# Running sums of logarithms as a float16 and a float32r product in a gated-recurrence kernel

## The chip, the cores and the metric

The kernel runs on one NeuronCore of one Trainium2 chip. The metric is the device time of one execution in microseconds (us). The engines are called by the names of the profile: PE (TensorE; its weight loads are PEld), DVE (VectorE), ACT (ScalarE), POOL (GpSimd) and SP (SyncE, which here only issues DMAs). They run side by side, each in the order of its own instructions, and wait for each other through semaphores.

## The reference, cut to what matters

```python
# 4 batches, 8 heads, 768 tokens, head dimension 48
for t in range(S):
    state = alpha[:, :, t, :, None] * state + einsum('bhd,bhe->bhde', k[:, :, t], v[:, :, t])
    y[:, :, t] = einsum('bhd,bhde->bhe', q[:, :, t], state)
x = y.transpose(0, 2, 1, 3).reshape(3072, 384)
# mixture of experts: 8 experts, 384 -> 1024 -> 384, each row to one expert
logits = x @ w_gate
expert_idx = argmax(logits, axis=1)            # gate_w: that expert's softmax value
for e in range(8):                             # rows sorted by expert
    y_sorted[lo:hi] = maximum(x_sorted[lo:hi] @ w1[e], 0) @ w2[e]
return gate_w[:, None] * y_sorted[inv_perm]
```

The decay `alpha` lies between 0.8 and 1. The product of the decays from one token to another is computed as the exponential of a difference of running sums of logarithms. These running sums are what the change touches.

## The kernel before, in words

The first stage is the recurrence. The 768 tokens are cut into 6 chunks of 128, and a step handles one chunk of one of the 4 batches, all 8 heads at once: 24 steps, of which step `i` has chunk `i // 4` and batch `i % 4`. The second stage is the mixture of experts, one expert after another; the change does not touch it. The order of the instructions of each engine is the order in which the code writes them (`manual_schedule`), so a step's place in the loop at lines 670 to 746 of the program is also its place in each engine's queue.

For a tile `s` (one chunk of one batch) the stage does this:

- `load` (L380): SP issues the loads of `a`, `k`, `q`, `v`, most of them for two tiles at once (384 KB). `loads_for(i)` at the start of a step issues those that fall due: `a` up to the tile whose sum is taken four steps later, `v`, `k` and `q` three and five tiles ahead. The `a` tiles have 4 buffers, `k` and `q` 3.
- `logs` (L388, ACT): `lna`, the logarithm of `a`, 128x384.
- `cums` (L393, PE; L396 and L397, ACT): one float32 matmul with the constant 128x128 matrix `cum_m` (0, 1 and -1) gives the running sums, taken from the middle of the chunk, in the PSUM bank `cum`. ACT reads it twice: `icp` is the exponential of its negative, `cp` its exponential.
- `decay_out` (L410, DMAs from ACT's queue) brings one row of `icp` and `cp` to the four-row tiles `dec`. `decay_rows` (L418, L419, POOL) multiplies them into the first 4 of the 128 rows of `er`, whose other rows stay zero. `decay_cols` (L430, PE) turns `er` by four transposes against the identity, into a bank that shares the tag `cum`; DVE copies the four columns that matter to `E` (L432).
- `operands` (L439, POOL): `k` times `icp` and `q` times `cp`, to one of three buffers `kqb`.
- `transposes` (L449, PE): eight transposes of `kqb`; copied out as `kT` and `qT` by ACT and DVE (L453, L455).
- `scores` (L462, PE), `mask` (L470, DVE: `dA`, `dB`), `scale_state` (L477, POOL: the state times `E`, called `U`), `read_state` (L489, PE), `attend` (L499, PE), `keys_values` (L510, PE), `result` (L518, ACT: `yT`), `add_state` (L528, DVE: `acc`), `rows` (L536, PE: `x`, output and logits in one bank), `logits` (L543, L544, DVE), `gate` (L550, ACT: `gex`), `keep_rows` (L561, ACT: `xs`; L562, SP's store to `x_rows`).

In step `i` PE runs, in this order: scores of `i`; in steps 4, 8, 12, 16 and 20 the four transposes of `decay_cols`; the eight transposes of `i+1`; the running sums of tile `i+5` (while there are tiles left: steps 2 to 18 have one); read_state, attend and keys_values of `i`; rows of `i-1`. ACT runs `yT` of `i-1`, `gex` of `i-2`, the logarithm of tile `i+5`, `kT` of `i+1`, `icp` and `cp` of tile `i+5`, `xs` of `i-2`, and issues the DMAs of `decay_out`. DVE runs logits, `acc`, in decay steps `E`, the two masks, `qT`, the gate weight, and the routing work that `route(i)` gives it. POOL runs operands of `i+2`, `U` of `i+1` or `decay_rows`, and from step 13 on one-hot rows (L291, L292).

Of the kernel before, what the change touches and what calls it, by code (L numbers as in the profile page):

```python
# [7 lines left out]

F32 = mybir.dt.float32
F16 = mybir.dt.float16  # L10
I32 = mybir.dt.int32
U16 = mybir.dt.uint16
AX = mybir.AxisListType.X
AF = mybir.ActivationFunctionType
ALU = mybir.AluOpType
# [4 lines left out]
def kernel(  # L20
# [29 lines left out]
    nc = tc.nc  # L50
    B, H, S, D = q.shape
    C = 128
# [4 lines left out]
    Dm = H * D  # L57
# [4 lines left out]
    D2 = 2 * D  # L62
    DP = 64
    HC = C // 2
    assert NB * C == S and FB * C == F and DB * C == Dm and D <= DP


# [16 lines left out]
    consts = ctx.enter_context(tc.tile_pool(name="consts", bufs=1))  # L84
    ident = consts.tile([C, C], F32)
    cmask = consts.tile([C, C], F32)
    cum_m = consts.tile([C, C], F32)
    kqb = [consts.tile([C, 2, NP, 2, DP], F32, name=f"kqb{i}") for i in range(3)]
    er = consts.tile([C, NP, 2, DP], F32)

# [9 lines left out]
            nc.vector.memset(t[:, :, :, :, D:], 0.0)  # L100

    def second_consts():
        nc.vector.tensor_scalar_mul(iw[:, :, D2:], iw[:, :, D2:], -1.0)
        for i in range(2):
            nc.vector.tensor_copy(
                iw[i * DP : (i + 1) * DP, :, i * D : (i + 1) * D],
                ident[i * DP : (i + 1) * DP, None, i * DP : i * DP + D].to_broadcast([DP, NP, D]),
            )
# [6 lines left out]
    for name, shape, pattern, base, mult in (  # L115
# [9 lines left out]
        iotas[name] = (  # L125
            consts.tile(shape, I32, name=name + "_i"), consts.tile(shape, F32, name=name), pattern, base, mult,
        )
    first_w, key0, thr, kx, first, cols, iota_f, tokv = (iotas[n][1] for n in iotas)
    iota_r = consts.tile([C, C], F16)
    iota_c = consts.tile([C, NC], F16)  # L130

# [94 lines left out]
    early = ctx.enter_context(tc.tile_pool(name="early", bufs=1))  # L226
    oh_r = sm.tile([C, NT, C], F16)
    oh_c = sm.tile([C, NT, NC], F16)

# [50 lines left out]
    def rows_cols(g_):  # L280
        ts = slice(g_ * TG, (g_ + 1) * TG)
        tr, ti = small("tr", (C, TG)), small("ti", (C, 3, TG), I32)
        nc.vector.reduce_sum(tr[:], pr[g_].rearrange("p e t -> p t e"), axis=AX)
# [21 lines left out]
    def place_experts():  # L305
# [17 lines left out]
        nc.vector.reduce_sum(xf[:], aw[:], axis=AX)  # L323
        xe = small("xe", (1, E), I32)
        nc.vector.tensor_copy(xe[:], xf[:])
        pd.update(end=end, place=place, at=at, xe=xe)

    def decode(v, n, name, pool=None):
# [3 lines left out]
        u, gf, sf = (pool.tile([C, n], F32, name=name + k_) for k_ in "ugs")  # L332
        gi, si = (pool.tile([C, n], I32, name=name + k_) for k_ in ("gi", "si"))
        nc.vector.tensor_scalar(gf[:], v, scalar1=0.0, scalar2=float(N + 1), op0=ALU.is_lt, op1=ALU.mult)
# [4 lines left out]

        qb, qf = pool.tile([C, 2, n], I32, name=name + "qb"), pool.tile([C, 2, n], F32, name=name + "qf")  # L340
        nc.vector.tensor_scalar(sf[:], u[:], scalar1=0.0, scalar2=float(2 * N), op0=ALU.is_lt, op1=ALU.mult)
# [22 lines left out]
    with tc.tile_pool(name="ld", bufs=6) as ld, \  # L364
         tc.tile_pool(name="work", bufs=2) as work, \
         tc.tile_pool(name="ps", bufs=1, space=PSUM) as ps:
        st = {s: {} for s in range(NT)}
# [18 lines left out]
        def logs(s):  # L386
            t = work.tile([C, Dm], F32, name="lna", bufs=4)
            nc.scalar.activation(t[:], st[s]["a"].rearrange("s h d -> s (h d)"), AF.Ln)  # L388
            st[s]["lna"] = t

        def cums(s, bank="cum"):
            cum = ps.tile([C, 512], F32, name="cum", tag=bank)
            nc.tensor.matmul(cum[:, :Dm], lhsT=cum_m[:], rhs=st[s]["lna"][:], start=True, stop=True)  # L393
            cp = work.tile([C, Dm], F32, name="cp", bufs=6)
            icp = work.tile([C, Dm], F32, name="icp", bufs=6)
            nc.scalar.activation(icp[:], cum[:, :Dm], AF.Exp, scale=-1.0)  # L396
            nc.scalar.activation(cp[:], cum[:, :Dm], AF.Exp)  # L397
            st[s]["cp"], st[s]["icp"] = cp, icp
# [25 lines left out]
        def pair(t, p):  # L424
            return t[:, p].rearrange("s a d -> s (a d)")

        def decay_cols(c):
            ep = ps.tile([C, NP, C], F32, name="ep", tag="cum")
            for p in range(NP):
                nc.tensor.transpose(ep[:, p, :], pair(er[:], p), ident[:])  # L430
            decay[c] = work.tile([C, NP, B], F32, name="E", bufs=2)
            nc.vector.tensor_copy(decay[c][:], ep[:, :, :B])  # L432

# [96 lines left out]
        def rows(s):  # L530
# [3 lines left out]
            for m in range(NP):  # L534
                for o in (0, HC):
                    nc.tensor.matmul(  # L536
# [28 lines left out]
        def do(f, i, *a):  # L565
            if 0 <= i < NT:
                f(i, *a)
# [4 lines left out]
        def sums_to(i):  # L572
            return {-2: 1, -1: 1, 0: 3, 1: 5}.get(i, -1 if i < 0 else min(i + 5, NT - 1))

        def new_sums(i):
            return range(sums_to(i - 1) + 1, sums_to(i) + 1)

        loaded = dict(a=0, k=0, q=0, v=0)

        singly = {-5: "aakq", -4: "kqav", -3: "akq", -2: "aav", -1: "kq", 0: "avakq", 1: "vkq"}  # L580
# [5 lines left out]
        def loads_for(i):  # L586
            for n in singly.get(i, ""):
                load_next(n, 1)
            if i > 1:
                for n, upto in ("a", sums_to(i + 4)), ("v", i + 3), ("k", i + 5), ("q", i + 5):  # L590
                    while loaded[n] <= min(upto, NT - 1):
                        load_next(n, 2)

# [70 lines left out]
        def route(i):  # L664
            for f, *args in on_vector.get(i, ()):
                if f is slots:
                    args[1] = counted(args[1])
                f(*args)

        for i in range(-4, NT):  # L670
            loads_for(i)
            do(scores, i)
            if i < NT - 1:
                do(result, i - 1)
            do(logits, i - 2)
            if i >= B:
                do(add_state, i - 1)
            do(gate, i - 2)
            if i > 0:
                for s in new_sums(i):  # L680
                    logs(s)
            if i == NT - 1:
                early_turn()
            if 0 < i < NT and i % B == 0:
                decay_cols(i // B)
            do(mask, i, 0)
            do(mask, i, 1)
            if i < B:
                do(add_state, i - 1)
            do(transposes, i + 1)  # L690
            sums = list(new_sums(i))
            for s in sums[:1]:
                cums(s)
            if i < 0:
                for s in sums[1:]:
                    cums(s, "x")
            do(gate_weight, i - 2)
            route(i)
            do(keep_rows, i - 2)
            if len(sums) == 1:  # L700
                decay_out(sums[0])
            if i == -1:
                for s in range(2):
                    decay_out(s)

            if B - 1 <= i < 2 * B - 1:
                decay_out(i + 1, (1,))
            if i == NT - 2:
                si = next(se)[1]
                eg["si"] = lambda j, r: si[:r, j : j + 1]  # L710
            if i == B:
                scale_state(i)
            do(operands, i + 2)
            if i > B and i % B == 0:
                scale_state(i)
            if 0 < i + 1 < NT and (i + 1) % B == 0:
                decay_rows((i + 1) // B)
            elif i >= 0:
                do(scale_state, i + 1)
            one_hots(nc.gpsimd, *on_gpsimd.get(i, ()))  # L720
            do(read_state, i)
            do(attend, i)
            if i == NT - 2:
                result(i)
            if i >= 0 and sums[1:]:
                cums(sums[1])
                for s in sums:
                    decay_out(s, (0,) if i else (0, 1))
            do(keys_values, i)
            if i == NT - 3:  # L730
                held["tok"] = ps.tile([C, NC], F32, name="tok", tag="cum")
                tokens(held["tok"][:], *range((NG - 1) * TG))
                se = early_gather()
            do(rows, i - 1)
            if i in counts_in:
                counts(counts_in[i], counted(i - 1))
            if i < 0:
                for s in new_sums(i + 1):
                    logs(s)
            if i == -3:  # L740
                second_consts()
            if i in (-4, 0, 1):
                for j in {-4: (0, 1, 2), 0: (3,), 1: (4,)}[i]:
                    late_consts(j)
            if 12 <= i < 22:
                fetch_part(groups[0], i - 12)
# [541 lines left out]
    with tc.If(nx > 0):  # L1288
        with tc.For_i(0, nx, 1) as i:
            ex = nc.sync.value_load(xi[0:1, bass.ds(i, 1)], min_val=0, max_val=E - 1)  # L1290
            col = wk.tile([C, 1], F32, name="col")
            nc.vector.tensor_copy(col[:], xx[:, 1, bass.ds(i, 1)])
            m = wk.tile([C, NT], F16, name="m")
            nc.vector.scalar_tensor_tensor(
# [41 lines left out]
```

## Time and profile before

| What | Before |
|---|---|
| Runs, us | 406.01 median (405.68, 406.01, 410.5) |
| Profiled execution, us | 405.81 |
| Its span, first to last instruction, us | 404.1 |
| PE busy, share of the span | 390.1 us, 97% |
| ACT, DVE, POOL busy | 54%, 51%, 36% |
| Mean granted PE clock | 0.988 |
| Matmuls of `cum` (L393) | 48 records, median 488 ns |
| Transposes of `er` (L430) | 20 records, median 273 ns |

A record is one pass of PE. Every float32 matmul of the table shows as two records, a float32 transpose as one. [...]what a pass costs in a dense stretch is read from start to start. In views named by a line (L393 is line 393 of the program), `out<-in` gives the tiles written and read, `x2` the number of records merged, and the bracket at the end the idle time of the engine before it and what ended it. A view by windows gives, for stretches of time, each engine's busy time with its number of instructions, the granted clock, the share of the DMA engines' time and the rate in GB/s. The recurrence takes the span up to some 146 us, the experts the rest.

### The profile page before, as it was taken

How to read it: one execution, taken by the hardware profiler on the slowest of the kernel's cores; microseconds unless marked ns; L12 is line 12 of the kernel's file. 1: busy time of each engine (PE TensorE's matmuls, PEld its weight loads, DVE VectorE, ACT ScalarE, POOL GpSimd, SP SyncE). 2: the span in 40 equal slices, each digit the busy share in tenths (PEclk: the TensorE clock that was granted, in tenths of full speed). 3: DMA queues.
4: the chain of work that ended last, by engine and by line, in shares of the span. 5: the costliest groups of instructions: out<-in, count | busy, mean ns of one | idle time of the engine just before them, and what ended most of it. 6: DMA issues, size and time to landing. Idle time of an engine off the chain costs nothing. (4 is left out here: it accounts for less than half of the span.)

```text
span 404.1 us, 9032 instructions
## 1 busy us (share of the span) xinstructions
PE 390.1 (97%) x3390; PEld 328.9 (81%) x3390; DVE 207.2 (51%) x636; ACT 219.6 (54%) x502; POOL 147.4 (36%) x203
## 2 busy tenths in 40 slices
PE   7999999999999999969999999999999999999994
PEld 4668888888888885859979978988978979979852
DVE  5554545664575665283692483473473483461200
ACT  5565556566665440112665666666666666763640
POOL 5447454688668203770005007007007003012031
PEclk9999999999999999979999999999999999999998
DMA  9999999999874315879346766865856965711311
GB/s 173 188 201 223 195 221 202 227 210 213 202 191 125 118 42 190 300 211 194 88 156 148 195 195 132 246 185 139 246 151 173 237 201 123 189 22 54 58 56 54
DMA packets 153905, 67.44 MB, mean 167 GB/s; under 512 B 136699, under 2 KB 148082, under 8 KB 153860
## 3 DMA queue, kind: packets, MB, share of 16 engines
q1 hardware_dynamic: 148756, 57.13, 59.0%
q0 software_dynamic: 3408, 9.64, 8.4%
q8 instruction: 27, 0.44, 0.5%
q10 hardware_dynamic: 1696, 0.08, 0.3%
q14 instruction: 18, 0.15, 0.1%
HBM read 49.00 MB, written 9.58 MB: 145 GB/s over the span
## 5 line engine op out<-in xcount | busy, mean ns | idle before, releaser
L1021 POOL DMA_INDIRECT out_dram<-zo,sp x25 | 26.0, 1041 | 137.5 <-ACT zo L1046 127.3
L185 DVE TENSOR_TENSOR h_sb<-pB,u 128x208 f32<-128x208 f32 (+6 forms) x56 | 20.2, 360 | 53.4 <-PE pB L909 39.5
L439 POOL TENSOR_TENSOR kqb<-k_sb,icp 128x384 f32<-128x384 f32 x23 | 23.0, 1000 | 36.8 <-PE y L510 17.0
L991 PE MATMUL pC<-h_sb,w 128*128 128x416 f32 (+5 forms) x96 | 33.9, 496 | 0.0
L851 ACT COPY u<-pA 128x208 f32<-128x208 f32 (+6 forms) x68 | 21.2, 312 | 18.5 <-PE pA L974 11.5
L909 PE MATMUL pA<-t,s 128*128 128x208 f32 (+6 forms) x112 | 28.6, 337 | 0.8
L462 PE MATMUL sA<-qT,kT 48*128 48x128 f32 x192 | 27.7, 284 | 0.9 <-DVE qT L453 0.9
L462 PE MATMUL sB<-qT,kT 48*128 48x128 f32 x192 | 27.7, 285 | 0.0
L909 PE MATMUL pA<-xgT,w 128*128 128x208 f32 (+6 forms) x112 | 27.7, 329 | 0.0
L449 PE MATMUL tp<-ident,kqb 128*128 128x128 f32 x192 | 25.9, 278 | 0.6 <-DVE kqb L439 0.6
L793 POOL DMA_INDIRECT xg<-x_rows,gp x25 | 23.9, 956 | 6.9 <-issue 6.8
L991 PEld LDWEIGHTS pC<-h_sb,w 128*128 128x128 f32 x96 | 18.0, 190 | 10.3 <-issue 3.7
L462 PEld LDWEIGHTS sA<-qT,kT 48*128 48x128 f32 x192 | 23.1, 187 | 3.8 <-ACT kT L455 1.1
L543 DVE TENSOR_REDUCE lgn<-x 128x8 f32<-128x32 f32 x23 | 4.4, 191 | 38.3 <-PE x L536 33.4
L920 ACT ACTIVATE h_sb<-h_sb 128x208 f32<-128x208 f32 (+6 forms) x28 | 10.3, 368 | 25.2 <-DVE h_sb L185 22.0
L909 PE MATMUL pB<-t,w 128*128 128x208 f32 (+6 forms) x112 | 23.8, 335 | 0.0
L439 POOL TENSOR_TENSOR kqb<-q_sb,cp 128x384 f32<-128x384 f32 x23 | 23.1, 1004 | 1.4 <-DMA q_sb<-in_q_dram 1.0
L449 PEld LDWEIGHTS tp<-ident,kqb 128*128 128x128 f32 x192 | 20.8, 140 | 3.4 <-issue 1.2
L909 PE MATMUL pC<-xgT,w 128*128 128x208 f32 (+6 forms) x112 | 23.1, 329 | 0.0
L462 PEld LDWEIGHTS sB<-qT,kT 48*128 48x128 f32 x192 | 23.1, 187 | 0.0
L518 ACT COPY yT<-y 128x512 f32<-128x512 f32 x24 | 14.1, 587 | 15.6 <-PE y L510 10.2
L470 DVE TENSOR_TENSOR dA<-sA,cmask 128x512 f32<-128x512 f32 x24 | 16.5, 689 | 11.3 <-PE sB L462 11.1
(256 smaller groups left out, 995.4 us busy)
## 6 DMA issues: line engine op xcount, KB each, us to landing
w<-in_moe_w_dram SPq DMA_DIRECT2D x14, 1536.0 KB
x_rows<-xs SPq DMA_DIRECT2D x24, 192.0 KB
v_sb<-in_v_dram SPq DMA_DIRECT2D x10, 384.0 KB
k_sb<-in_k_dram SPq DMA_DIRECT2D x9, 384.0 KB
q_sb<-in_q_dram SPq DMA_DIRECT2D x9, 384.0 KB
a_sb<-in_alpha_dram SPq DMA_DIRECT2D x8, 384.0 KB
a_sb<-in_alpha_dram SPq DMA_DIRECT2D x8, 192.0 KB
w<-in_moe_w_dram SPq DMA_DIRECT2D x6, 256.0 KB
```

Of the source, the lines that this page charges most:

```text
L185: eng.tensor_tensor(out, a, b, op=ALU.add)
L439: eng.tensor_tensor(by_half(kq[:, i]), d[n].rearrange("s (a p) d -> s a p d", a=2), d[e][:].rearrange("s (a p d) -> s a p d", a=2, p=NP), ...
L449: nc.tensor.transpose(tp[:, p, :], pair(kqb[s % 3][:, i], p), ident[:])
L462: nc.tensor.matmul(t[:, p, :], lhsT=d["kT"][r : r + D, p, :], rhs=d["qT"][r : r + D, p, :], start=True, stop=True,)
L470: nc.vector.tensor_tensor(t[:], d["sc"][i][:], cmask[:, None, :].to_broadcast([C, NP, C]), op=ALU.mult)
L518: nc.scalar.copy(d["yT"][:], y[:, :, : 2 * C].rearrange("r g (j t) -> r g j t", j=2))
L793: nc.gpsimd.indirect_dma_start(out=g["xg"][:r, j, :], out_offset=None, in_=x_d[:, :], in_offset=bass.IndirectOffsetOnAxis(ap=g["gi"](j, r) ...
L851: nc.scalar.copy(t[:, :m], bank["A"][:, :m])
L909: nc.tensor.matmul(out, lhsT=ops[n_][0], rhs=ops[n_][1], start=first and n_ == names[0], stop=True, skip_group_check=True,)
L920: nc.scalar.activation(out(0, 0), out(0, 0), AF.Relu)
L991: nc.tensor.matmul(d2[:, :n], lhsT=w2[:, f, 2 * C :], rhs=h[:, f, :n], start=(f == 0), stop=(f == FB - 1),)
L1021: ins = nc.gpsimd.indirect_dma_start(out=out[:, :], out_offset=bass.IndirectOffsetOnAxis(ap=g["si"](j, r), axis=0), in_=zo[:r], in_offset= ...
```

## The change

For tiles 11 to 23, whose sums fall in steps 6 to 18, the float32 product is split. ACT writes `hi`, the logarithm times 512 rounded to float16, right after the logarithm. DVE writes `lo`, the logarithm minus `hi`/512, as float32r, at the end of the step's routing work. PE adds two products in the bank: `hi` with `cum_h` (`cum_m`/512 in float16) and `lo` with `cum_r` (`cum_m` in float32r). So that DVE has a step for it, the logarithm and `hi` of these tiles are taken one step before the sum, not in the same step; step 5 takes two logarithms, of tiles 10 and 11. The loads of `a` come one step sooner from step 4 on. `decay_cols` turns only the four rows of `er` that hold data, so the moving identity is 4x4 and an output is 128x4. Two constants are made in `second_consts`, on DVE, before the first step.

```diff
+F32R = mybir.dt.float32r
...
+    APART, HS = 11, 512.0
...
+    cum_r = consts.tile([C, C], F32R)
+    cum_h = consts.tile([C, C], F16)
...
     def second_consts():
+        nc.vector.tensor_copy(cum_r[:], cum_m[:])
+        nc.vector.tensor_scalar_mul(cum_h[:], cum_m[:], 1.0 / HS)
...
             nc.scalar.activation(t[:], st[s]["a"].rearrange("s h d -> s (h d)"), AF.Ln)
             st[s]["lna"] = t
+            if s >= APART:
+
+                st[s]["hi"] = work.tile([C, Dm], F16, name="hi", bufs=2)
+                nc.scalar.mul(st[s]["hi"][:], t[:], HS)
+
+        def low_part(s):
+
+            t = st[s]["lo"] = work.tile([C, Dm], F32R, name="lo", bufs=1)
+            nc.vector.scalar_tensor_tensor(
+                t[:], in0=st[s]["hi"][:], scalar=-1.0 / HS, in1=st[s]["lna"][:], op0=ALU.mult, op1=ALU.add,
+            )
 
         def cums(s, bank="cum"):
             cum = ps.tile([C, 512], F32, name="cum", tag=bank)
-            nc.tensor.matmul(cum[:, :Dm], lhsT=cum_m[:], rhs=st[s]["lna"][:], start=True, stop=True)
+            if s < APART:
+                nc.tensor.matmul(cum[:, :Dm], lhsT=cum_m[:], rhs=st[s]["lna"][:], start=True, stop=True)
+            else:
+                nc.tensor.matmul(cum[:, :Dm], lhsT=cum_h[:], rhs=st[s]["hi"][:], start=True, stop=False)
+                nc.tensor.matmul(cum[:, :Dm], lhsT=cum_r[:], rhs=st[s]["lo"][:], start=False, stop=True)
...
             for p in range(NP):
-                nc.tensor.transpose(ep[:, p, :], pair(er[:], p), ident[:])
+                nc.tensor.transpose(ep[:, p, :B], pair(er[:B], p), ident[:B, :B])
...
+        def new_logs(i):
+            return [s for j in (i, i + 1) for s in new_sums(j) if (s >= APART) == (j > i)]
+
...
-                for n, upto in ("a", sums_to(i + 4)), ("v", i + 3), ("k", i + 5), ("q", i + 5):
+                for n, upto in ("a", sums_to(i + 4 + (i > 3))), ("v", i + 3), ("k", i + 5), ("q", i + 5):
...
-                for s in new_sums(i):
+                for s in new_logs(i):
                     logs(s)
...
             route(i)
+            for s in new_logs(i):
+                if s >= APART:
+                    low_part(s)
             do(keep_rows, i - 2)
```

## The prediction

> **What bounds the kernel now.** I read the page first, for the engine that is never idle.
>
> ```profile
> PE 390.1 (97%) x3390; PEld 328.9 (81%) x3390; DVE 207.2 (51%) x636; ACT 219.6 (54%) x502; POOL 147.4 (36%) x203
> PE   7999999999999999969999999999999999999994
> PEclk9999999999999999979999999999999999999998
> ```
>
> The first 14 digits of 40 (10.1 us each) are the recurrence. PE is at 90% or more there but for the first slice. [...]I then took windows whose edges are the first score matmul of each step. These are steps 18 and 19, the last with a running sum and the first without.
>
> ```profile
> core 0: us, PE busy (x) PEld busy (x) DVE busy (x) ACT busy (x) POOL busy (x), PEclk, DMA share, GB/s
> 111.12:116.57 5.45, 5.45 (x91) 4.46 (x91) 3.83 (x18) 3.81 (x9) 1.88 (x3) 1.00 0.63 164
> 116.57:121.36 4.79, 4.79 (x90) 4.19 (x88) 3.25 (x9) 2.55 (x6) 4.71 (x7) 1.00 0.91 225
> ```
>
> Step 18 takes 5.45 us and step 19 4.79. The timeline of PE says where the 0.66 lies (column one is the start):
>
> ```profile
> 112.22 1.09 PE L449 MATMUL tp<-ident,kqb 128*128 128x128 f32 x8
> 113.14 0.81 PE L393 MATMUL cum<-lna,cum_m 128*128 128x384 f32 x2
> 113.89 0.66 PE L489 MATMUL y<-qT,U 48*48 48x128 f32 x16
> ...
> 117.66 1.09 PE L449 MATMUL tp<-ident,kqb 128*128 128x128 f32 x8
> 118.68 0.65 PE L489 MATMUL y<-qT,U 48*48 48x128 f32 x16
> ```
>
> From transposes to read_state it is 1.67 us with the sum and 1.02 without: the sum alone costs 0.65, and nothing else moved. Steps 6, 7, 9, 10, 13, 14 and 15 also take 5.44 to 5.45. So PE's own instructions set the step, and a step without any sum is shorter by the whole of it. What is taken from the sum is taken from the time, until another engine's chain ends later.
>
> The nearest of these is ACT's. Step 14 begins at 88.36:
>
> ```profile
> 89.20 0.51 ACT L388 ACTIVATE lna<-a_sb 128x384 f32<-128x384 f32 x1
> 90.15 0.59 ACT L455 COPY kT<-tp 128x512 f32<-128x512 f32 x1 [0.44 <-PE tp L449]
> 91.29 0.49 ACT L396 ACTIVATE icp<-cum 128x384 f32<-128x384 f32 x1 [0.56 <-PE cum L393]
> 91.68 0.48 ACT L397 ACTIVATE cp<-cum 128x384 f32<-128x384 f32 x1
> 92.05 0.59 ACT L561 ACTIVATE xs<-x,gw 128x384 f32<-128x384 f32 x1
> ```
>
> ACT waits twice for PE: 0.44 us before `kT`, 0.56 before `icp`. `xs` must be done before the next rows, which write the same single bank `x`: it ends at 92.64, rows start at 92.98.
>
> [...]the sum is two records of some 0.32 us each (0.65 together)[...]. No float32r stands in it. [...]
>
> **The change part by part.** *The sum.* One product of 0.644 us becomes two[...]. The second weight load (190 ns as a record[...]) begins while the first product streams, as it does now. That saves 0.32 per step, times 13 steps: 4.2 us. Bounds: at the rate of one float32 pass, 0.32 for the float32r part, it saves 0.16, 2.1 us in all; at two passes it costs 0.16 more than now, 2.1 us. I take the full rate[...].
>
> *The four transposes.* Steps 12 and 16 against their neighbours: 5.89 against 5.44, 0.44 for four transposes, 0.11 each. The moving side shrinks from 128 to 4 columns; the load remains.
>
> ```profile
> L430 PEld LDWEIGHTS ep<-ident,er x20: 138/141/144, 33.1 to 122.7; 128*128 128x128 f32 x20
> L430 PE MATMUL ep<-ident,er x20: 272/273/332, 33.1 to 122.8; 128*128 128x128 f32 x20
> ...
> L393 PEld LDWEIGHTS cum<-lna,cum_m x48: 186/190/337, 4.2 to 113.1; 128*128 128x128 f32 x48
> ```
> ```profile
> 71.04 0.30 PEld L266 LDWEIGHTS x<-pr,lt_strict 128*128 128x128 f32 x2
> 71.26 0.30 PEld L266 LDWEIGHTS x<-pr,ones_sq 128*128 128x128 f32 x2
> ```
>
> L266 moves 8 columns and still needs 0.11 us a record (two in 0.22): its loads set the pace. A transpose's load is 50 ns shorter (141 against 190), so I put its pace at 0.06: four take 0.24, a gain of 0.20. Against that stands a seam: going from scores to transposes costs PE 0.1 us, and the next eight transposes use all rows again. I take 0.12 per decay step, five of them: 0.6 us. Bounds: 0.20 without a seam (1.0), and 0.44 + 0.1, a loss of 0.1 each (-0.5).
>
> *ACT.* `hi` adds one instruction of 0.51 (the row of `lna`) per step right after the logarithm. It fills the 0.44 before `kT`; `kT` starts 0.05 to 0.1 later, and `icp`, which PE releases 0.32 earlier, still finds ACT free because back-to-back instructions overlap by some 0.1. `xs` waits for the gate weight of DVE, ready at 91.70 here, so it can move up 0.3 with `cp`; rows move up 0.32 too. The margin of 0.34 stays within 0.1. Step 18 has 3.81 us of ACT, with `qT` on it; plus 0.51 that is 4.3 of 5.13. Step 5 gets a logarithm and `hi`, 1.0 us, against the same 0.44; its `icp` waits for PE anyhow and is late by at most 0.3. Uncovered, `hi` would cost 0.5 a step. Zero.
>
> *DVE.* `lo` is one 128x384 instruction; DVE's `kqb` product of that size takes 0.56. It is queued ahead of the next step's `lgn`, before which DVE sits idle 1.4 us at the end of step 13 and 2.2 at that of step 14; behind it wait `gex` and the masks. In step 12, which has routing work, DVE is free from some 81.9 to `lgn` at 83.0, so 0.56 fits; the fullest, step 18, gets none. Zero; 0.5 a step if the cover were gone. The two constants, 0.25 each by the copy to `cum_m` (0.24), fall in DVE's 1.03 us of waiting for `iw` at 3.9.
>
> *The earlier logarithm* takes the wait for `lna` off the sum: PE's only idle time put down to it is 0.6 us at 28.1, before the changed steps, so nothing. *The earlier loads:* from step 4 each pair of `a` is issued one step sooner on SP's queue, ahead of a store of `x_rows` that nobody reads before the gathers at 131, and of the small `alpha` row. The next pairs of `v`, `k` and `q` stood behind it already. A pair takes some 1.7 us (384 KB at 225 GB/s). POOL shows when loads were late:
>
> ```profile
> 55.46 1.00 POOL L439 TENSOR_TENSOR kqb<-q_sb,cp 128x384 f32<-128x384 f32 x1 [0.69 <-DMA q_sb<-in_q_dram]
> 59.65 1.00 POOL L439 TENSOR_TENSOR kqb<-k_sb,icp 128x384 f32<-128x384 f32 x1 [2.25 <-PE y L510]
> ```
>
> Up to step 8 POOL waits for loads, 4.8 us before PE needs their product; after it, for PE. The `k` pair of tiles 20 and 21 is issued at 94.39 and first read at 110.07. Two steps move 1.97 MB; in 10.25 us that is 192 GB/s, from step 12 on with two weight pieces of 0.26 MB 243, where windows of 5 us show up to 264. Zero. *POOL* is full in steps 13 and 14 (5.45 of 5.45), with one-hot rows nobody waits for; `decay_rows` ends at 97.45, PE needs it at 100.3. The cut takes 0.3 a step of this 2.9. Zero.
>
> **Sum.** 4.2 + 0.6 = 4.8 us. The profiled execution is 405.81 (span 404.1 and 1.7 around it), so 401.0; it stands 0.2 below the median of 406.01, to which the forecast is **401.2**. The experts' stage is PE-bound but for two gaps and shifts as a whole.
>
> **The rivals.** *Float32r is slower than I take it.* For it: no row shows it. Half rate gives 406.0 - 2.1 - 0.6 = 403.3; two passes 407.5. *The gain is absorbed,* by ACT through `xs` and the bank `x`, or by the loads: the DMA share is near 1.00 in most windows of the recurrence. Then steps stay at 5.45: 405.4. Against it are the margins above. *The clock.* PE idles twice for 1.6 us at 172.6 and 174.7, and the granted clock halves from 175.8 to 182.7, which costs 3.4 us. All this comes 4.8 us earlier[...]: half of it gone gives 399.5, all 397.8, half more 402.9. *Slower:* the scaling by 512 is not in the table set that ACT holds. The one load of a table here takes 1.28 us (L569); two per step and `hi` make 3.1, ACT's 3.81 becomes 6.9, and ACT sets the period: 1.45 x 13 = 19 us, 424. It decides from 1.6 us added to ACT (5.45 - 3.81). Against it: exponential, logarithm, copy with scale and Relu all run on that one load.
>
> **How the numbers follow.** Forecast 0.66 (400.2 to 402.3); float32r slower 0.12; absorbed 0.07; clock 0.10, of which 0.03 under 398; table 0.03; else slower 0.02. A measurement of this kernel tells about 2% from no change, 8.1 us: faster (below 397.9) 0.03, slower 0.04 (the table and half of the last case), within 0.93. The range goes from half of the clock's gain with the best transposes (399.5 - 0.4) to the half rate with the worst (403.3 + 1.1): 399.1 to 404.4. It leaves out the absorbed case, the two-pass rate, the whole clock's gain, the table and the rest, some 0.18.
>
> **What would show it.** Steps 13 to 15 at 5.13 us; `cum` as two records 0.16 apart with read_state 0.42 after the first; decay steps at 0.3 above their neighbours; ACT's wait before `kT` gone, that before `icp` left; steps 19 to 23 as before. The prediction is wrong if the second record lasts 0.32, if PE shows waits before rows or read_state, or if the throttle's stretch has another length.

## The result and the profile after

| | before | after |
|---|---|---|
| time, median of 7 runs | 406.01 us (404.14 to 410.5) | 401.72 us (401.12 to 403.01) |
| profiled execution | 405.81 | 402.5 |
| its span | 404.1 | 400.8 |
| an ordinary step with a running sum (9, 11, 13 to 15) | 5.44 to 5.45 | 5.13 to 5.14 |
| decay steps 12 and 16 | 5.89 | 5.47 |
| step 8, a decay step too | 5.89 | 5.95 |
| stretch at half clock in the experts | 6.83 from 175.8 | 6.83 from 172.5 |

The ratio is 0.988, interval 0.9842 to 0.9918, which is 3.3 to 6.4 us. The ratios here leave disturbed runs out, so they are not always the quotient of the medians. Times of this kernel differ from chip to chip (before had 406.01, 402.85, 408.28 and 402.34 us on the four used here), so a variant is compared with before on its own chip only. The change was repeated on two more chips and gave 0.9895 and 0.9881 there.

The page first: PE's row, then PE and its granted clock in 40 slices. Everything looks as it did.

```profile
PE 386.0 (96%) x3390; PEld 328.2 (82%) x3390; DVE 213.8 (53%) x651; ACT 224.8 (56%) x515; POOL 148.4 (37%) x203
PE   7999999999999999979999999999999999999994
PEclk9999999999999999969999999999999999999998
```

The count of PE's instructions is the same, 3390: a float32 matmul was already two records, and now the two are a float16 and a float32r one. PE's busy time fell by 4.1 us (390.1 to 386.0); ACT gained 13 instructions and 5.2 us, DVE 15 and 6.6. What became of that is seen in windows from one step's first score matmul to the next one's, here steps 8, 14, 16, 18 and 19 of after.

```profile
core 0: us, PE busy (x) PEld busy (x) DVE busy (x) ACT busy (x) POOL busy (x), PEclk, DMA share, GB/s
53.84:59.79 5.95, 5.55 (x96) 4.77 (x94) 3.30 (x10) 4.01 (x10) 4.19 (x6) 1.00 1.07 244
86.34:91.47 5.13, 5.13 (x93) 4.45 (x91) 3.21 (x9) 3.73 (x10) 5.13 (x8) 1.00 0.87 193
96.61:102.08 5.47, 5.47 (x97) 4.76 (x95) 3.30 (x10) 3.92 (x9) 5.28 (x9) 1.00 1.08 215
107.75:112.88 5.13, 5.13 (x91) 4.45 (x90) 3.83 (x18) 3.29 (x8) 1.87 (x3) 1.00 1.02 233
112.88:117.68 4.80, 4.80 (x91) 4.19 (x89) 3.28 (x9) 2.55 (x6) 4.72 (x7) 1.00 0.90 240
```

Step 19, without a sum, stays at 4.80. A step with one is now 0.34 longer than that; it was 0.66 longer. PE is busy all through every step here but step 8, where 0.40 us are missing (5.55 of 5.95). Inside step 14, on PE:

```profile
87.43 1.09 PE L472 MATMUL tp<-ident,kqb 128*128 128x128 f32 x8
88.36 0.33 PE L415 MATMUL cum<-hi,cum_h 128*128 128x384 f16 x1
88.39 0.47 PE L416 MATMUL cum<-lo,cum_r 128*128 128x384 f32 x1
88.79 0.66 PE L512 MATMUL y<-qT,U 48*48 48x128 f32 x16
```

From transposes to read_state it is 1.36 us; in the kernel before it was 1.67. And on ACT, in the same step:

```profile
87.18 0.51 ACT L396 ACTIVATE lna<-a_sb 128x384 f32<-128x384 f32 x1
87.71 0.52 ACT L401 ACTIVATE hi<-lna 128x384 f16<-128x384 f32 x1
88.14 0.57 ACT L478 COPY kT<-tp 128x512 f32<-128x512 f32 x1
88.95 0.49 ACT L419 ACTIVATE icp<-cum 128x384 f32<-128x384 f32 x1 [0.24 <-PE cum L416]
89.34 0.48 ACT L420 ACTIVATE cp<-cum 128x384 f32<-128x384 f32 x1
89.71 0.58 ACT L584 ACTIVATE xs<-x,gw 128x384 f32<-128x384 f32 x1
```

`hi` stands where the wait before `kT` was. The wait before `icp` is left, with 0.24 of its 0.56 us. `xs` ends at 90.29, the rows that need its bank start at 90.64.

**The account of the two profiled executions.** The span fell by 3.3 us. Thirteen sums at 0.31 are 4.0. The transposes are worth 0.10 in step 4, 0.11 in 8, 12 and 16 each (0.42 less the 0.31 of the sum; in step 8 taken alike) and 0.19 in step 20: 0.6. Step 3 is 0.1 shorter. Against these 4.7 us stand step 8 with 0.5, step 5 with 0.2, the start with 0.15 (first scores at 8.95 instead of 8.80) and a wait of 0.6 for the first gather, in step 23. That leaves 3.3. The change was profiled twice more, as after_again and after_third, on other chips. Of the four losses step 8's comes back in both, and step 5's in neither (5.44 and 5.45). The wait for the gather comes back in one: 0.82 us in after_third, none in after_again. It also stands in three variants of the change (0.28 to 0.57) and in neither of the two profiled kernels with the old sums, so whether the change pays for it stays open. First scores come at 8.80 to 9.43 in all kernels, so the start is scatter. Without step 5, the start and the gather the account is 4.6 - 0.5 = 4.1 us. The median fell by 4.3, and by 4.5 and 3.9 on the other two chips; with an interval of 3.3 to 6.4 this agreement is no test of the account, and the steps are the evidence.

The wait of step 8, on PE:

```profile
55.27 1.09 PE L472 MATMUL tp<-ident,kqb 128*128 128x128 f32 x8
56.20 0.33 PE L415 MATMUL cum<-hi,cum_h 128*128 128x384 f16 x1
56.23 0.47 PE L416 MATMUL cum<-lo,cum_r 128*128 128x384 f32 x1
57.11 0.65 PE L512 MATMUL y<-qT,U 48*48 48x128 f32 x16 [0.40 <-POOL U L500]
```

And what POOL did up to then:

```profile
52.57 0.99 POOL L441 TENSOR_TENSOR er<-dec 4x384 f32<-4x384 f32 x1 [2.36 <-issue]
53.64 1.01 POOL L442 TENSOR_TENSOR er<-er,alpha 4x384 f32<-4x384 f32 x1
54.62 1.00 POOL L462 TENSOR_TENSOR kqb<-k_sb,icp 128x384 f32<-128x384 f32 x1
55.59 1.00 POOL L462 TENSOR_TENSOR kqb<-q_sb,cp 128x384 f32<-128x384 f32 x1
56.55 0.97 POOL L500 TENSOR_TENSOR U<-acc,E 128x192 f32<-128x192 f32 x2
```

The last line holds two instructions of 0.5 us, `U` of step 8 and then `U` of step 9. The first is done at about 57.05, and PE asks for it at 56.71. In the kernel before, POOL and then PE:

```profile
51.63 0.99 POOL L418 TENSOR_TENSOR er<-dec 4x384 f32<-4x384 f32 x1 [1.31 <-issue]
...
56.42 0.99 POOL L477 TENSOR_TENSOR U<-acc,E 128x192 f32<-128x192 f32 x2
```
```profile
57.47 0.66 PE L489 MATMUL y<-qT,U 48*48 48x128 f32 x16
```

There `U` of step 8 was done at about 56.9 and PE asked at 57.47: 0.5 us to spare. So PE came 0.76 us earlier and POOL did not. `er`, which opens the row of five, even started 0.94 later; `U` is only 0.15 later, as before had a gap of 0.69 in the row, for the load of `q` (the line at 55.46 in the prediction), and after has none.

### The profile page after: what moved, and what is told of

The parts are those of the page before. It is cut to its first block, busy times and chain, and to the rows that moved or that the text cites. A ratio compares the mean times of both kernels' runs of the same rounds, so it can differ in the third digit from the quotient of the medians.

```text
span 400.8 us, 9107 instructions
## 1 busy us (share of the span) xinstructions
PE 386.0 (96%) x3390; PEld 328.2 (82%) x3390; DVE 213.8 (53%) x651; ACT 224.8 (56%) x515; POOL 148.4 (37%) x203
## 4 chain that ended last, share of the span: by engine, by line
PE 64%; issue 22%; POOL 5%; DMA 3%; DVE 2%; ACT 2%; POOLq 0%; ACTq 0%; DVEq 0%
PE pA L938 7%; PE pC L1020 5%; PE tp L472 5%; PE pB L938 5%; PE sA L485 5%; PE y L522 5%; PE pA L1003 4%; PE x L559 4%; PE pA L1181 3%; POOL out_dram L1050 3%; PE y L512 2%; PE pC L938 2%; PE cum L413 2%; PE pA L1209 2%; PE pB L1003 2%
## 5 line engine op out<-in xcount | busy, mean ns | idle before, releaser
L193 DVE TENSOR_TENSOR h_sb<-pB,u 128x208 f32<-128x208 f32 (+6 forms) x56 | 20.2, 360 | 53.3 <-PE pB L938 39.4
L938 PEld LDWEIGHTS pA<-t,s 128*128 128x128 f32 x112 | 19.1, 189 | 3.3 <-ACT u L880 2.1
```

The lines of the kernel that those rows point to most:

```text
L193: eng.tensor_tensor(out, a, b, op=ALU.add)
L938: nc.tensor.matmul(out, lhsT=ops[n_][0], rhs=ops[n_][1], start=first and n_ == names[0], stop=True, skip_group_check=True,)
```

## The experiments

### One part at a time: e1_sums_only and e2_turns_only

The change with the four old transposes:

```diff
-                nc.tensor.transpose(ep[:, p, :B], pair(er[:B], p), ident[:B, :B])
+                nc.tensor.transpose(ep[:, p, :], pair(er[:], p), ident[:])
```

> The changed kernel with the four transposes of the decay rows as before (all 128 rows). Theory (PE's own instructions set the step): steps with a sum 5.14 us, decay steps 0.44 above their neighbours in place of 0.33, so 0.11 x 5 = 0.55 us slower than the changed kernel, some 402.2. Rival (the gain is mostly that of the transposes, or of the order of the loads): nearer to 404 or above.

And the kernel before with the four new ones, the same edit the other way round:

> The kernel before with four rows turned, sums in one float32 product. Theory: decay steps 0.33 above their neighbours, which stay at 5.45; 0.55 us faster than before, some 405.4. Rival (a seam or a wait for the decay eats it): no difference from before in the decay steps, or slower ones.

| same chip, before 402.85 | ratio | ordinary step | steps 12 and 16 | four transposes |
|---|---|---|---|---|
| e1_sums_only, 398.51 | 0.9888 (0.9843 to 0.9934) | 5.13 to 5.14 | 5.57 | 0.43 |
| e2_turns_only, 402.67 | 0.9991 (0.9961 to 1.0021) | 5.45 (step 13: 5.50) | 5.78 | 0.34 |

The split sums alone give the whole of what the time shows. The transposes give 0.10 to 0.11 per decay step, the same with and without the sums, and five of them can't be seen in a time. Why so little: the transposes of after and of e1_sums_only as one tile's instructions, minimum, median and maximum in ns.

```profile
L453 PEld LDWEIGHTS ep<-ident,er x20: 133/136/138, 33.2 to 119.0; 4*128 4x128 f32 x20
L453 PE MATMUL ep<-ident,er x20: 197/198/220, 33.2 to 119.0; 4*128 4x4 f32 x20
```
```profile
L453 PEld LDWEIGHTS ep<-ident,er x20: 138/141/143, 35.3 to 122.3; 128*128 128x128 f32 x20
L453 PE MATMUL ep<-ident,er x20: 272/273/328, 35.3 to 122.4; 128*128 128x128 f32 x20
```

The load of 4 rows takes 136 ns where that of 128 takes 141, so fewer rows hardly shorten it. In step 8 of after the four start at 54.94, 55.02, 55.08 and 55.14, some 0.06 us apart, and the eight of 128 rows follow 0.13 after the last.

### What each of the two products costs: e3_hi_alone and e4_f32r_alone

The first runs the float16 product alone, the second the float32r product alone, with the whole logarithm as its operand:

```diff
# e3_hi_alone
-                nc.tensor.matmul(cum[:, :Dm], lhsT=cum_h[:], rhs=st[s]["hi"][:], start=True, stop=False)
-                nc.tensor.matmul(cum[:, :Dm], lhsT=cum_r[:], rhs=st[s]["lo"][:], start=False, stop=True)
+                nc.tensor.matmul(cum[:, :Dm], lhsT=cum_h[:], rhs=st[s]["hi"][:], start=True, stop=True)
# e4_f32r_alone
-                t[:], in0=st[s]["hi"][:], scalar=-1.0 / HS, in1=st[s]["lna"][:], op0=ALU.mult, op1=ALU.add,
+                t[:], in0=st[s]["hi"][:], scalar=0.0, in1=st[s]["lna"][:], op0=ALU.mult, op1=ALU.add,
...
-                nc.tensor.matmul(cum[:, :Dm], lhsT=cum_h[:], rhs=st[s]["hi"][:], start=True, stop=False)
-                nc.tensor.matmul(cum[:, :Dm], lhsT=cum_r[:], rhs=st[s]["lo"][:], start=False, stop=True)
+                nc.tensor.matmul(cum[:, :Dm], lhsT=cum_r[:], rhs=st[s]["lo"][:], start=True, stop=True)
```

> The changed kernel without the float32r product; the float16 product alone makes the sums, DVE still writes the low part. This leaves out the low part of the sums. It measures what the float32r product costs PE. [...]steps fall from 5.14 to 4.98. If it streams at the rate of a float32 pass (0.32 us), steps fall to 4.82 and the float16 product would have to be almost free.

> The changed kernel without the float16 product; the low part is the whole logarithm in float32r. This leaves out the exact split, the sums have float32r precision. If each product costs 0.16 us, steps fall from 5.14 to 4.98, as in the run without the float32r product. If float32r costs 0.32 and float16 almost nothing, steps stay at 5.11 to 5.14.

PE's timeline in step 14, of e3_hi_alone and then of e4_f32r_alone:

```profile
90.86 1.09 PE L471 MATMUL tp<-ident,kqb 128*128 128x128 f32 x8
91.78 0.33 PE L415 MATMUL cum<-hi,cum_h 128*128 128x384 f16 x1
92.04 0.66 PE L511 MATMUL y<-qT,U 48*48 48x128 f32 x16
```
```profile
89.87 1.09 PE L471 MATMUL tp<-ident,kqb 128*128 128x128 f32 x8
90.72 0.42 PE L415 MATMUL cum<-lo,cum_r 128*128 128x384 f32 x1
91.07 0.66 PE L511 MATMUL y<-qT,U 48*48 48x128 f32 x16
```

From transposes to read_state it is 1.18 and 1.20 us, where both products take 1.36. The steps agree: 4.96 without the float32r product and 4.97 without the float16 one, against 5.14. So float32r costs 0.18 and float16 0.17, together the 0.34 by which a step with a sum exceeds step 19. That settles the rate: over 384 columns float32r takes what float16 does, to some 0.01 us. It also settles how the two records of after are to be read. They start 0.03 us apart (88.36 and 88.39), but each takes its full share of the step, 0.17 and 0.18: the distance of these two starts is not the cost of a product. The two kernels took 399.31 and 398.38 us, one run each, too close to each other and to the change for a reading of their own. (e4_f32r_alone waits 2.01 us at read_state in step 8; the section on that wait comes back to it.)

### How much ACT can still take: e6_hi_twice and e7_hi_thrice

The scaling is done twice or three times into the same tile, 0.55 us more each time:

```diff
                 nc.scalar.mul(st[s]["hi"][:], t[:], HS)
+                nc.scalar.mul(st[s]["hi"][:], t[:], HS)
+                nc.scalar.mul(st[s]["hi"][:], t[:], HS)   # e7_hi_thrice only
```

> The changed kernel with the scaling to hi written twice, 0.55 us more of ACT in each of 13 steps. From the run with three scalings (1.1 us more, steps 0.50 longer), ACT's margin behind the one scaling is about 0.6 us: steps 9 to 16 stay at 5.14 and 5.47. Rival (the margin is much smaller): steps longer by 0.2 to 0.5.

> The changed kernel with the scaling to hi written three times in place of once, 1.04 us more of ACT in each of 13 steps. Theory (ACT has some 0.5 us to give before xs is late for the rows): xs ends at 4.6 us of the step, rows start at 4.65 in place of 4.30, steps with a sum take about 5.45. Rival 1 (ACT already sets the step): 6.1 to 6.2. Rival 2 (ACT is nowhere near): 5.14 unchanged.

Their times, one run each, were 397.52 us (before 402.34 on that chip) and 411.77 (before 408.28). With twice, steps 9 and 11 to 16 keep their 5.13 to 5.14 and 5.47, and step 10 its 5.67 to 5.68. Step 17, where ACT has `qT` as well, goes from 5.67 to 6.12, and step 7 from 5.14 to 5.45; in both PE waits for `xs` before the rows. With thrice, steps 9, 11 and 13 to 15 take 5.63 to 5.65, and so do the decay steps 8, 12 and 16. ACT and then PE in step 14 of e7_hi_thrice:

```profile
95.94 0.57 ACT L480 COPY kT<-tp 128x512 f32<-128x512 f32 x1
96.40 0.49 ACT L421 ACTIVATE icp<-cum 128x384 f32<-128x384 f32 x1
96.79 0.49 ACT L422 ACTIVATE cp<-cum 128x384 f32<-128x384 f32 x1
...
97.16 0.59 ACT L586 ACTIVATE xs<-x,gw 128x384 f32<-128x384 f32 x1
```
```profile
96.97 0.53 PE L535 MATMUL y<-v_sb,kqb 128*48 128x48 f32 x16
97.80 0.93 PE L561 MATMUL x<-iw,yT 128*64 128x104 f32 x16 [0.30 <-ACT xs L586]
```

The wait before `icp` is gone, `xs` ends at 97.75, and the rows wait for it. This is the rival "absorbed by ACT through `xs` and the bank `x`", made to happen. 1.10 us more cost 0.50 a step, so the cover behind `hi` is 0.6 us. It is the sum of two lines of after: the 0.24 that `icp` still waits and the 0.35 from the end of `xs` to the rows. The expectation of 5.45 was too low; the mechanism and the place were right.

### Where the wait of step 8 comes from

**after_again**, the change unaltered on another chip, and **e5_loads_as_before**, with the loads of `a` back at their old step:

```diff
-                for n, upto in ("a", sums_to(i + 4 + (i > 3))), ("v", i + 3), ("k", i + 5), ("q", i + 5):
+                for n, upto in ("a", sums_to(i + 4)), ("v", i + 3), ("k", i + 5), ("q", i + 5):
```

> The changed kernel once more, to see which of its waits come back. Theory: steps with a sum 5.14, decay steps 5.47, and in step 8 read_state late again by 0.3 to 0.5 us (step 8 at 5.8 to 5.95), because tile 10's loads land no earlier while PE asks 0.8 us earlier. Rival (chance of one run): step 8 at 5.47. The wait for the early gather in step 23 (0.59 us) is expected to vary.

> The changed kernel with the loads of a at the step in which the kernel before has them. If the moved loads cause the wait in step 8 (rival), step 8 falls to 5.47 and the run gains 0.5 us on the changed kernel. If the rate of the loads causes it and the moved load adds only some 0.1 (theory), step 8 stays at 5.7 to 5.85 and the time is the same within 0.3 us. No step gets slower, as a is ready several us before it is read.

**e8_loads_later** goes further and takes those loads later than the logarithms can bear, `sums_to(i + 2 + (i > 3))` in the same line:

> The changed kernel with each pair of a from tile 10 on issued behind one more pair of k and q than now. Theory (steps 3 to 8 wait for k and q, which share one queue with a): k and q of tiles 6 to 11 land 1.7 us sooner, step 8 at 5.47, the other steps as in the changed kernel; 0.4 to 0.7 us faster than it. Rival (ACT, by the logarithm of step 5, is what delays): step 8 unchanged, or the logarithms come late and steps 5 to 8 get longer.

| same chip, before 408.28 | ratio | step 6 | step 8 | wait at read_state of step 8 |
|---|---|---|---|---|
| after_again | 0.9895 (0.9847 to 0.9944) | 5.14 | 6.16 | 0.62 |
| e5_loads_as_before | 0.9876 (0.9824 to 0.9929) | 5.13 | 6.87 | 0.62, and 0.64 at the four transposes |
| e8_loads_later | 0.991 (0.9879 to 0.994) | 7.17 | 5.47 | none |

The wait is there again, and giving the loads back does not remove it. So the moved loads are not its cause, nor the operands of tile 10 being late for want of their loads, as I had written for after_again: POOL in e5_loads_as_before runs `er` to `U` without a gap. Late loads can add to the wait, though: in e4_f32r_alone POOL stands still for 1.03 and 0.27 us ahead of the two operand products, the second time for the load of `q`, and `U` starts at 57.87 when PE had asked at 56.74. In e8_loads_later the late logarithm is seen instead, on ACT and then PE:

```profile
47.13 0.52 ACT L396 ACTIVATE lna<-a_sb 128x384 f32<-128x384 f32 x1 [2.52 <-DMA a_sb<-in_alpha_dram]
```
```profile
49.98 0.94 PE L559 MATMUL x<-iw,yT 128*64 128x104 f32 x16 [1.83 <-ACT xs L584]
```

Step 6 loses 1.83 us to it, as the rival had it, and step 8 has no wait. PE comes to step 8 that much later, so this run cannot tell whether earlier `k` and `q` would have done it too. These runs fit one reading: it matters only whether PE or POOL's row of five is first at `U`.

**e9_state_first** tests that reading. In step 8 POOL is given `U` before the operands of tile 10, as it already was in step 4:

```diff
-            if i == B:
+            if i in (B, 2 * B):
...
-            if i > B and i % B == 0:
+            if i > 2 * B and i % B == 0:
```

> The changed kernel with the state of step 8 scaled on POOL ahead of the operands of tile 10, as step 4 has it. Theory (the decay rows of tile 8 come late because the row DMAs of step 6 land late, and U of step 8 then stands on POOL behind two operand products of 1.0 us each): step 8 at 5.47 in place of 5.95 or more, the operands of tile 10 two thirds of a us later but still 2 us before PE turns them; 0.5 us faster than the changed kernel on this chip. Rival (late k and q loads): step 8 stays above 5.8, or the wait moves to the transposes of step 9.

**after_third** is the change unaltered on the same chip:

> The changed kernel on the chip of these runs, to compare them with. Theory: steps with a sum 5.14, decay steps 12 and 16 at 5.47, step 8 late by 0.3 to 0.8 with POOL busy without a gap from the decay rows to U.

POOL in e9_state_first:

```profile
52.21 1.06 POOL L441 TENSOR_TENSOR er<-dec 4x384 f32<-4x384 f32 x1 [2.35 <-issue]
53.35 1.00 POOL L442 TENSOR_TENSOR er<-er,alpha 4x384 f32<-4x384 f32 x1
55.30 0.52 POOL L500 TENSOR_TENSOR U<-acc,E 128x192 f32<-128x192 f32 x1 [0.96 <-DVE E L455]
55.77 1.01 POOL L462 TENSOR_TENSOR kqb<-k_sb,icp 128x384 f32<-128x384 f32 x1
56.74 1.00 POOL L462 TENSOR_TENSOR kqb<-q_sb,cp 128x384 f32<-128x384 f32 x1
```

`U` starts at 55.30, 1.0 us before read_state starts at 56.30, and POOL now waits 0.96 us for `E` instead of PE waiting for POOL. Step 8 takes 5.47, what steps 12 and 16 take, and no wait stands at step 9's transposes. In after_third it takes 6.00, with 0.46 of waiting. The cause is shown: the order on POOL. Why `er` starts so late can be read from the traces, though the views put POOL's 2.36 us before it down to no releaser. ACT's queue sends rows by three DMAs at 47.01 to 48.79 in after (46.83 to 48.62 in before), and `er` of step 8 needs the last of them. By the semaphore records of the traces this DMA signals its end at 52.45 in after and at 51.42 in before, and `er` starts 0.12 and 0.21 us later; in all 14 profiled executions it is 0.12 to 0.21. So `er` waits for its rows. In after, 15 of the 16 signals of that DMA have come by 51.34, and the last comes 1.1 us behind them. Such a straggler, of 1.1 to 1.4 us, is in five of the twelve profiles of the change and its variants and in neither of the other two; what holds it up is not known.

**e10_state_first_from10** adds to e9_state_first that the sum of tile 10, in step 5, is split too: `APART, HS = 10, 512.0`.

> The same, with the split sums from tile 10 on, so that step 5 has one too and the double logarithm falls in step 4. Theory: step 5 at 5.14 in place of 5.45, step 4 as before or up to 0.2 longer; 0.1 to 0.3 us faster than the run without it. Rival (the early steps are held by loads and row DMAs): the 0.31 of step 5 comes back as a wait in steps 6 to 8.

| same chip, before 402.34 | median | ratio | step 5 | step 8 |
|---|---|---|---|---|
| after_third | 398.44 (396.39 to 400.72) | 0.9881 (0.9824 to 0.9938) | 5.45 | 6.00 |
| e9_state_first | 396.54 (395.55 to 402.63) | 0.9871 (0.9802 to 0.9941) | 5.45 | 5.47 |
| e10_state_first_from10 | 398.44 (395.57 to 402.21) | 0.9886 (0.9856 to 0.9916) | 5.13 | 5.67 |

The last one gains 0.32 in step 5 and gives 0.2 of it back in step 8, where `er` ends at 55.14 and the four transposes start only at 55.19. Neither is measurably faster than the change; the 0.5 us of e9_state_first is shown in the step alone.

## Why the prediction was right, and where not

**The bound.** "PE's own instructions set the step" held: in steps 9, 11 and 13 to 15 the step fell by what PE's sum lost, 0.31 us, in every kernel with both products and ACT's single scaling. One reading was wrong, at no cost: step 10 took 5.99 us in before, not 5.44 to 5.45, as it has the counting products of L266 besides; it fell by 0.31 too.

**The sum, 4.2 us.** 13 times 0.31 are 4.0. The choice that carried it was to take each of the two products at half of one float32 pass. Before has no float32r product, and its float16 ones have 32 columns (L299), so for 384 columns this was my estimate, which the runs bear out. The float32r product measured 0.18 us for 384 columns, by the step of e3_hi_alone, and the float16 one 0.17, by that of e4_f32r_alone; one float32 pass takes 0.32 in before, half of the 0.65 of its sum. The rival of half the rate (403.3) and that of two passes (407.5) fall with it.

**The four transposes, 0.6 us.** 0.10 to 0.11 a decay step instead of 0.12, and 0.19 in step 20, which has no sum; why that one gives more stays open. The pace of 0.06 and a seam of 0.13 are both in the trace.

**ACT, zero.** Right: `kT` starts 0.01 later in the step (88.14 less 86.34, against 90.15 less 88.36) where 0.05 to 0.1 was allowed, `icp` and `xs` 0.32 earlier, the margin at the bank is 0.35. Two slips that cost nothing. What ACT has left after one `hi` is 0.6, not 0.34, since the wait of `icp` adds to it. And `hi` never falls into step 18, as I reckoned: logarithms run a step ahead now, so step 18 has 3.29 us of ACT, and step 17 is the full one, with 4.12.

**DVE, zero.** PE never waited for `lo`, and the steps that also have routing work, 10, 12 and 17 among them, fell by as much as the others.

**Step 5** was allowed 0.3 for `icp`, at no net cost; it lost 0.21 in the profiled execution and nothing in after_again and after_third.

**POOL, zero: the term that was mis-sized.** It measured 0.5 us (0.40 to 0.62 of waiting), lost. I looked at `decay_rows` in steps 13 to 16, where POOL has over 2 us to spare, and had found for the steps up to 8 that the operands are ready 4.8 us before PE needs them. I didn't ask what is queued behind these operands on POOL: `U` of the same step, with 0.5 us to spare. That `er` could start a further 0.94 later, with its rows, was not weighed either. I had the cut of 0.3 a step in hand and did not add it up over steps 6 to 8. One of the signs that I gave for a wrong prediction, a wait before read_state, did occur, in this one step.

**The loads, zero.** e5_loads_as_before does not show the old place to be better; e8_loads_later shows that two steps later is too late.

**The clock.** The stretch kept its length, 6.83 us, in the two profiled executions, and moved forward by 3.3 us with the rest of the stage. In the other kernels, the unaltered change among them, it is not always there: the clock of e9_state_first is a 9 in all 40 slices, where after has a 6, and the six runs of after_third have mean clocks from 0.993 to 1.000. The runs of before on the chip of e9_state_first have mean clocks from 0.992 to 1.000 too; a stretch of 6.83 us at half clock takes 0.0085 from a mean over 403 us, so by this estimate before runs both with and without it. So this rival is a scatter between runs, which the change does not decide. That the two profiled executions had the same stretch was luck.

**A sign that was wrong.** "Two records 0.16 apart": they are 0.03 apart, and the products take 0.17 each all the same. Read_state 0.42 after the first was right: 0.43.

The sum came out at 4.6 less 0.5, where 4.8 was said, and the median fell by 4.3. The mechanism held; that the median came within 0.5 us of the forecast is in part luck, with an interval as wide as 3.3 to 6.4 us.

## What to carry to other kernels

Where PE was busy all through a step (5.45 of 5.45 us in step 14 of before), a cut of its work was worth its full length, 0.31 us. Where one engine is that busy, count a cut in full, but add the cut up over the steps and compare it with every margin on the way, also with that of what stands *behind* an early instruction in another engine's queue. Take the cost of an operation from the distance of its neighbours with and without it, not from the distance of two records' starts (0.17 and 0.18 against 0.03 here). Reordering two instructions of an engine that has time (POOL's `U` ahead of operands for two steps later) can take such a wait away; in e9_state_first no other step got longer for it.

## What the runs showed of the hardware that I had not expected

**Stretches of half clock follow long idling of PE, not always.** The one in the experts lasts 6.83 us in before and in after, at 0.50 of the clock. Each stretch seen, but for the last microseconds of an execution, began within about 2 us of a gap on PE of 1.6 us or more (at 175.8 in before and 172.5 in after, in the second of two gaps: 1.58 and 1.62 us in before, 1.51 and 1.64 in after; at 30 in e2_turns_only, in a gap of 2.35). A gap of up to 1.2 us by itself was never followed by one (1.05 us in e9_state_first); some of 1.83 to 2.58 us were not either (2.58 in e1_sums_only at 28.3, with a clock of 1.00 throughout the stages that followed). So the length of a gap alone does not decide; what else does is not shown.

**Where one stall of DVE falls goes with whether these gaps appear in the experts.** DVE and then POOL in after, ahead of the stretch at 172.5:

```profile
168.12 0.14 DVE L1150 CAST xn<-ve 1x1 int32<-1x1 f32 x1
168.19 2.80 DVE L1152 TENSOR_TENSOR vb<-ve,nb 128x8 f32<-128x8 f32 x1
170.92 0.35 DVE L1155 TENSOR_TENSOR xa<-ve,kx 128x192 f32<-128x192 f32 x1
```
```profile
168.62 3.33 POOL L842 COPY xh<-xg 128x768 uint16<-128x768 uint16 x4
```

An instruction on 8 elements a partition lasts 2.80 us (L1166, on as many, takes 0.15 at 173.26), and ends at 170.99 where the third of POOL's four copies ends at 170.97. In before it is the same one, with 2.76 us. In e9_state_first a stall of 2.86 us falls on a later instruction, of 24 elements, PE idles once for 1.05 us, and no stretch follows. In e1_sums_only it is 2.96 us on yet another (`s`, L193, which takes 0.67 in e9_state_first), with one gap of 0.99 on PE and no stretch. All 14 profiles divide so. In six (before, after, after_again and three variants) the instruction held up beside the copies is `ve` or `vb`, PE then idles for 1.62 to 1.69 us, and the half clock follows. In eight it is a later one, `xx` or `s`, PE idles once for 0.99 to 1.05 us, and in the experts no stretch follows. Between after and e9_state_first lie some 2 us of idling (1.51 and 1.64 against 1.05) and 3.4 of clock (half of 6.83), more than the whole change brings, and before has it as after does. In all 14 profiles the instruction held up ends with the third copy or at most 0.6 us after it. In ten of the 14 DVE's record starts ahead of the first copy's (168.19 against 168.62 in after, 166.64 against 167.10 in e9_state_first, 171.40 against 171.44 in e1_sums_only), and yet DVE is the one held up. That the copies are the cause was not tried.

**The start of the recurrence scatters by more than the change.** PE waits in step 3 for the logarithm of its sum from nothing to 2.8 us, in kernels of both kinds, and step 3 takes 5.5 to 10.0 us. That is why steps were compared here and not spans. Its cause was not tried.
